# Score tiles as two runs of 64-row products, with a ScalarE copy before their search

## The chip, the core and the metric

The kernel runs on one NeuronCore of a Trainium2 chip. The metric is device time in microseconds of one execution. Five engines work side by side, each in the order of its own queue: TensorE (PE, matrix products; PEld is its weight load), VectorE (DVE), ScalarE (ACT), GpSimd (POOL) and SyncE (SP, which here issues most DMAs). They wait for each other through semaphores. Products are summed in PSUM, which has eight banks of 128 partitions by 512 fp32 values; everything else lies in SBUF or in DRAM.

## What is computed

The input x is 2048 rows of 512 values. With xn the row-wise normalised x, the output is x + A(xn) + B(xn):

- A is attention with 32 heads of 16 and one shared head of keys and values: scores, softmax over 2048 keys, weighted sum of values, output projection.
- B is a mixture of 4096 tiny experts with product keys: for each row and head, a query gives 64 scores against each of two key sets (k1, k2), the best two of each set are found, their four sums ranked, and the best two experts taken, with a softmax over two as gates. Each expert is one row of u and one row of v: `gelu(xn . u) * gate * v`, summed over heads.

The query weights and the keys are multiplied first, so the expert scores of a row are one product of xn with a 512 x 4096 matrix. Per row that gives 64 groups (32 heads, two sets) of 64 scores.

## The kernel before

**Units of work.** Rows come in 16 tiles of 128, four tiles to a phase (`TPH`). The 4096 score columns come in eight chunks of 512 (`NC`). `SEQ` (line 508) lists the 32 pairs of phase and chunk in the order in which they are scored: phase 0 whole, two chunks of phase 1, phase 2 whole, the rest of phase 1, phase 3 whole. For phases 0 and 1 the experts found are gathered from DRAM (a slot is one gathered expert for each of 128 rows: a dot at line 999, an add at line 1034). For phases 2 and 3 the experts are computed densely by `dense`, once the last chunk of the phase is scored.

**A score tile** is made by `item` (lines 513 to 549): twelve products of 128 contracted rows by 512 columns (four parts of the 512-long contraction, each with three terms of a high and low split), summed in one PSUM tile named psc. The weights are XT (xn transposed, one per phase group) and the moving operand WC (the chunk's matrix, tiles wk). Then VectorE searches the PSUM tile directly: eight MAX8 and eight FIND_INDEX8 (with their MATCH_VALUE_LOAD) over 64 columns each. After four tiles `batch` turns maxima and indices into expert numbers and gates.

**PSUM.** `xtile` (line 123) hands out one-bank tiles from a ring of three, to score tiles and to all other users: wp_make, block_out (pwo), the dense part (pact, pg, pout, ptd). `stile` hands out two pairs of banks for attention scores.

**Order.** From line 1255 on the order on every engine is written out by hand. The loop (line 1259) has 256 steps d, each with four calls of `scores` (attention scores, `sc`, line 327: two products of 64 contracted rows, in the upper and the lower half of the array, into two banks, and one exponential on ScalarE) and two of `pv` (line 341: products with 32 output columns). A step is emitted as: two scores, two pv, `mid` (VectorE's dots and adds, ScalarE's small functions, gathers), two scores, sometimes a `block_out` (four 128-row products of the output projection, pwo), then `fill`. `fill` runs a generator, `score_thread`, until the sum of the costs that it yields reaches a line that ends at FILL after 256 steps; three score products cost 3 x `UNIT` = 0.705. So a step has 15 or 18 score products. The generator also makes the chunks' matrices (`wp_make`, for chunks 0 to 7, done by the seventh chunk); later chunks are read back from DRAM (`wp_read`, tiles wk, eight buffers, two chunks). At a change of phase `load_xt` loads each tile's columns of XT after its last use.

The number of gather slots worked on in a step is set by `pos` (line 1267): 2.1 a step until phase 0 is searched, then 2.3 for twelve steps after a dense part and 1.75 otherwise, with rates of its own in the dense part.

Of the kernel before, what the change touches and what calls it, by code (L numbers as in the profile page):

```python
# [11 lines left out]
F32 = mybir.dt.float32  # L12
# [4 lines left out]
U32 = mybir.dt.uint32  # L17
# [6 lines left out]
P = 128  # L24
# [4 lines left out]
E = 64  # L29
# [3 lines left out]
KC = D // P  # L33
NC = 8
TPH = GT
# [6 lines left out]
NWK = 8  # L42
NIDX = 9
GS = 8192.0
FILL = 948.0
SCALE = DH ** -0.5
LIMIT2 = 25000.0
C_IN = 0.7978845608028654
# [3 lines left out]
UNIT = 0.235  # L52
# [3 lines left out]
def tile_kernel(ctx, tc, x, wq, wkv, wo, wqT, kT, uv, ub, vb, out):  # L56
    nc = tc.nc
# [4 lines left out]
    late = [None]  # L62
    start_stack = ExitStack()
    small = pool("small", bufs=2)
# [55 lines left out]
    nc.gpsimd.memset(ones_f, 1.0)  # L120

    gtile = lambda dt=F32, shape=(P, 1024), name="g": big.tile(list(shape), dt, name=name, tag="g", bufs=NGB)
    xtile = lambda name: ps.tile([P, 512], F32, name=name, tag="x", bufs=3)
    stile = lambda name: ps.tile([P, 2, 512], F32, name=name, tag="s")


# [375 lines left out]
    def wp_read(n, ks=range(KC)):  # L502
        for k in ks:
            wk = wk_tile()
            nc.sync.dma_start(raw(wk[:]), d_w[SEQ[n][1]][:, k])
            WC.setdefault(n, []).append(wk)
# [3 lines left out]
    M8, I8 = {}, {}  # L510
    BT = 4

    def item(n_, ti, make=()):
        ph, c = SEQ[n_]
        nph, nc_ = SEQ[n_ + 1] if n_ + 1 < len(SEQ) else (None, None)
        t = TPH * ph + ti
        g, j = divmod(t, GT)
        b, jb = divmod(ti, BT)
        if jb == 0:
            m8 = small.tile([P, BT, 8, 8], F32, name="m8", bufs=1)  # L520
            i8 = small.tile([P, BT, 8, 8], U32, name="i8", bufs=1)
            M8[ph, c, b], I8[ph, c, b] = m8, i8
        m8, i8 = M8[ph, c, b], I8[ph, c, b]
        p = xtile("psc")

        more = nc_ is not None and not (ph >= NSP and c == NC - 1)
        read = more and n_ + 1 >= NC
        n = 0
        for k in range(KC):
            for a, bb in TERMS:  # L530
                nc.tensor.matmul(p, XT[k][:, a, j * P:(j + 1) * P], WC[n_][k][:, bb, :],  # L531
                                 start=n == 0, stop=n == 11)
                n += 1
            if read and ti == 0 and k < 2:
                wp_read(n_ + 1, range(2 * k, 2 * k + 2))
            if k < KC - 1:
                yield 3 * UNIT
            if k == 1:

                yield from islice(make, 1)  # L540
        if more and nph != ph:
            load_xt(nph, j)
        for s in range(8):
            nc.vector.max(m8[:, jb, s, :], p[:, s * E:(s + 1) * E])  # L544
        for s in range(8):
            nc.vector.max_index(i8[:, jb, s, :], m8[:, jb, s, :], p[:, s * E:(s + 1) * E])  # L546
        if jb == BT - 1:
            batch(ph, c, b)
        yield 3 * UNIT

    IDX, G = {}, {}
# [544 lines left out]
        ACC[t], XN[t] = xa[:, 0, :], xa[:, 1, :]  # L1096
        LIVE.add(t)

    def load_xt(g, j=None, ks=range(KC)):
        c = slice(0, 512) if j is None else slice(j * P, (j + 1) * P)  # L1100
        for k in ks:
            nc.sync.dma_start(raw(XT[k][:, :, c]), d_xt[g - 1][k][:, :, c])

    def score_thread():
        for n, (ph, c) in enumerate(SEQ):
            if n < 2:
                yield from wp_make(c)
            make = wp_make(n + 1) if 0 < n < NC - 1 else iter(())
            dn = None
            if ph >= NSP and c == NC - 1:  # L1110
                dn = dense(ph, n + 1 if n + 1 < len(SEQ) else None)
                yield next(dn)
            for ti in range(TPH):
                if dn and ti == 1:
                    yield next(dn)
                if dn and ti == 2:
                    dense_on[0] = 4
                yield from item(n, ti, make)
                yield from islice(make, 1)
            yield from make  # L1120
            WC.pop(n)
            if ph >= NSP and c == NC - 1:
                yield from dn
                dense_on[0] = 0

# [129 lines left out]
    with tc.manual_schedule(engines={E_.PE, E_.Activation, E_.DVE, E_.Pool, E_.SP}):  # L1255
# [3 lines left out]
        for d in range(half + 24):  # L1259


            if dense_on[0] != 0:
                since = d
            if dense_on[0] == 1:
                pos += 2.6 if d < half * 3 // 4 else max(0.0, NSL - pos) / max(half - 3 - d, 1)
            else:
                pos += (2.1 if len(IDX) < NC * TPH else 2.3 if 0 <= d - since < 12 else 1.75, 0, 1.4, 1.5, 0.5)[dense_on[0]]

            todo = max(min(int(pos + 0.001), g_next[0]) - d_next[0], 0)

# [108 lines left out]
```

## Time and profile before

| | us |
|---|---|
| median of 3 runs | 1915.05 |
| lowest and highest run | 1909.74, 1916.33 |
| the profiled execution | 1918.82 |
| its span, first to last instruction | 1917.1 |

The profiler's record of one execution gives, for each instruction, its engine, its start and its length. Rows of the timeline show the start, the length, the engine, the line of the kernel, what is written and read, and how many equal instructions in a row were merged (x). `64*128` in a TensorE row means 64 contracted rows and 128 columns of the array. Rows of stretches show the start and end, the length, then the busy time and the number of instructions of each engine. Product lengths include the way through the array, so products that follow each other overlap in the record; the distance of their starts is what one costs.

### The profile page before, as it was taken

What the parts mean: (1) busy time and instruction counts of PE and PEld (TensorE: products, weight loads), DVE (VectorE), ACT (ScalarE), POOL (GpSimd) and SP (SyncE); (2) the same over time, 40 slices, a digit from 0 to 9 for tenths busy, and PEclk for the clock granted to TensorE, in tenths of its full rate; (3) what the DMA queues carried; (4) which work ended last, traced back from release to release, by engine and by line L of the source; (5) the groups of instructions that cost most, each with busy time, mean ns of one, the idle gap of its engine ahead of it and who ended that gap; (6) DMA issues with size and microseconds to landing.
All of it is one profiled execution on the core that took longest, in us unless ns stands there. A gap on an engine that the chain in (4) does not pass through costs nothing.

```text
span 1917.1 us, 35007 instructions
## 1 busy us (share of the span) xinstructions
PE 1822.9 (95%) x10990; PEld 961.5 (50%) x10990; DVE 1633.0 (85%) x6381; ACT 1290.6 (67%) x1803; POOL 693.8 (36%) x920
## 2 busy tenths in 40 slices
PE   6879999999999889999999999999998899999998
PEld 4544444555555344555555454555543345555553
DVE  6626888889998987999999797899989779999994
ACT  3236666655557987787877555555579777878773
POOL 1202334334443213343444354344522124444430
PEclk9989999999999999999999999999999899999999
DMA  7856878898673678898999987877646878899982
GB/s 264 312 191 235 293 267 289 286 296 282 232 261 111 223 245 259 250 288 274 284 289 307 340 283 234 290 244 264 229 129 220 263 222 292 267 285 280 295 265 79
DMA packets 245724, 489.76 MB, mean 255 GB/s; under 512 B 93972, under 2 KB 106644, under 8 KB 245532
## 3 DMA queue, kind: packets, MB, share of 16 engines
q0 software_dynamic: 73728, 268.47, 42.1%
q1 hardware_dynamic: 170568, 218.18, 35.0%
q8 instruction: 88, 1.44, 0.3%
q10 hardware_dynamic: 1236, 0.82, 0.1%
q14 instruction: 104, 0.85, 0.1%
HBM read 426.49 MB, written 55.61 MB: 251 GB/s over the span
## 4 chain that ended last, share of the span: by engine, by line
PE 76%; DVE 10%; DMA 3%; ACT 2%; issue 1%; SPq 1%; ACTq 0%; DVEq 0%
PE pv L341 20%; PE psc L531 18%; PE sc L327 15%; PE pact L733 9%; PE pout L872 9%; DVE oh L792 3%; PE pwo L434 2%; DVE xa L1034 2%; DVE g L999 1%; PE pw L487 1%; DVE oh L795 1%; ACT pt L330 1%; DVE oh L794 1%; DMA wqt<-in_wqT_dram 1%; DMA wk<-dw 1%
## 5 line engine op out<-in xcount | busy, mean ns | idle before, releaser
L330 ACT ACTIVATE pt<-sc 128x1024 f32<-128x1024 f32 x1024 | 994.6, 1028 | 449.1 <-PE sc L327 394.2
L987 POOL DMA_INDIRECT g<-in_uv_dram,idx x512 | 555.0, 1084 | 997.1 <-DVE xa L1034 518.3
L341 PE MATMUL pv<-pt,vaug 128*32 128x512 f32 x4096 | 499.4, 604 | 0.0
L327 PE MATMUL sc<-qa,kaug 64*128 64x512 f32 x2048 | 387.7, 451 | 15.7 <-ACT pt L330 14.1
L531 PE MATMUL psc<-wk,xt 128*128 128x512 f32 x1536 | 390.4, 402 | 8.0 <-DMA wk<-dw 4.4
L1034 DVE SCALAR_TENSOR_TENSOR xa<-g,w,xa 128x512 f32<-128x512 f32 x512 | 372.2, 745 | 0.1
L999 DVE CUSTOM_DVE_ANT_0 g<-g,xa 128x512 f32<-128x512 f32 x512 | 335.7, 682 | 6.2 <-DMA g<-in_uv_dram,idx 6.2
L531 PEld LDWEIGHTS psc<-wk,xt 128*128 128x128 f32 x1536 | 278.9, 189 | 111.8 <-issue 39.6
L327 PEld LDWEIGHTS sc<-qa,kaug 64*128 64x128 f32 x2048 | 157.4, 186 | 332.3 <-ACT pt L330 206.5
L341 PEld LDWEIGHTS pv<-pt,vaug 128*32 128x32 f32 x4096 | 107.7, 110 | 247.6 <-issue 246.0
L546 DVE FIND_INDEX8 i<-m,psc 128x8 uint32<-128x64 f32 x1024 | 206.6, 222 | 0.0
L733 PE MATMUL pact<-xt,wk 128*128 128x512 f32 x768 | 196.0, 400 | 0.0
L872 PE MATMUL pout<-wk,wd 128*128 128x512 f32 x768 | 194.9, 402 | 0.2 <-DVE wd L930 0.2
L544 DVE MAX8 m<-psc 128x8 f32<-128x64 f32 x1024 | 146.6, 215 | 41.3 <-PE psc L531 36.8
L872 PEld LDWEIGHTS pout<-wk,wd 128*128 128x128 f32 x768 | 140.8, 188 | 47.5 <-DVE act L999 5.5
L733 PEld LDWEIGHTS pact<-xt,wk 128*128 128x128 f32 x768 | 139.4, 188 | 48.5 <-issue 17.4
L875 DVE TENSOR_TENSOR da<-da,pout 128x512 f32<-128x512 f32 x128 | 82.9, 680 | 10.1 <-PE pout L872 6.6
L698 DVE TENSOR_TENSOR wk<-rw,wk 128x512 fp32r<-128x512 f32 x128 | 84.9, 684 | 6.7 <-ACT wk L697 6.7
L792 DVE TENSOR_TENSOR oh<-oh 128x2048 f16<-128x2048 f16 x64 | 78.0, 1219 | 0.6 <-ACT pt L330 0.4
L697 ACT CAST wk<-rw 128x512 fp32r<-128x512 f32 x128 | 74.1, 632 | 0.0
L546 DVE MATCH_VALUE_LOAD i<-m,psc 128x8 f32 x1024 | 72.6, 71 | 0.0
L1022 DVE SCALAR_TENSOR_TENSOR w<-gth,ga 128x4 f32<-128x4 f32 x128 | 20.5, 160 | 51.2 <-ACT gth L1015 50.6
(159 smaller groups left out, 1344.6 us busy)
## 6 DMA issues: line engine op xcount, KB each, us to landing
wk<-dw SPq DMA_DIRECT2D x96, 512.0 KB
wqt<-in_wqT_dram SPq DMA_DIRECT2D x32, 512.0 KB
dw<-wk SPq DMA_DIRECT2D x32, 512.0 KB
rw<-in_ub_dram SPq DMA_DIRECT2D x64, 256.0 KB
rw<-in_vb_dram SPq DMA_DIRECT2D x64, 256.0 KB
gy<-dg SPq DMA_DIRECT2D x64, 256.0 KB
qa<-dqh SPq DMA_DIRECT2D x128, 64.0 KB
g<-in_uv_dram,idx POOLq DMA_INDIRECT x512
```

Of the source, the lines that this page charges most:

```text
L327: nc.tensor.matmul(p[:, b, :], kaug[o:o + 64, kc * P:(kc + 1) * P], QA[u][o:o + 64, i, :], start=True, stop=True)
L330: nc.scalar.activation(pt, p, AF.Exp, scale=SCALE)
L341: nc.tensor.matmul(PV[u][32 * j:32 * j + 32, :], vaug[:, kc, :], pt[:, b, :], start=kc == 0, stop=kc == 15)
L531: nc.tensor.matmul(p, XT[k][:, a, j * P:(j + 1) * P], WC[n_][k][:, bb, :], start=n == 0, stop=n == 11)
L544: nc.vector.max(m8[:, jb, s, :], p[:, s * E:(s + 1) * E])
L546: nc.vector.max_index(i8[:, jb, s, :], m8[:, jb, s, :], p[:, s * E:(s + 1) * E])
L733: nc.tensor.matmul(p, us[:, a, k * P:(k + 1) * P], XT[k][:, c, :], start=n == 0, stop=n == 11)
L792: nc.vector.tensor_tensor(out=oa, in0=num(P), in1=bc(0, tb, P), op=OP.is_equal)
L872: nc.tensor.matmul(p, wd[0][:, a, j * P:(j + 1) * P], vs[:, c, :], start=n == 0, stop=n == 5)
L987: nc.gpsimd.indirect_dma_start(out=gt, out_offset=None, in_=uv, in_offset=bass.IndirectOffsetOnAxis(ap=IDX[ph, c, ti][:, s:s + 1], axis=0))
L999: nc.vector.tensor_tensor_reduce(u, u, XN[TPH * ph + ti], scale=1.0, scalar=0.0, op0=OP.mult, op1=OP.add, accum_out=a[:, i:i + 1])
L1034: nc.vector.scalar_tensor_tensor(acc, v, w[:, i:i + 1], acc, op0=OP.mult, op1=OP.add)
```

## The change

From the eighth chunk on (`n_ >= NC - 1`, 25 of 32 chunks) a score tile is an object `Halves`. Each of its twelve steps is two products of 64 contracted rows: the first run uses rows 0 to 63 and writes the tile's first sum, the second run uses rows 64 to 127 and adds to it. `first_half` issues a first-run step and queues its partner; once more than 18 (`LAG`) are queued, the oldest partner is issued right behind. So TensorE's queue alternates between a first-run product of one tile and a second-run product of an older tile, in another bank.

Between the runs of a tile stands a small ScalarE copy (`seen`): it waits for the last product of the first run, and the first product of the second run waits for it. At the end of the second run `done` copies the tile to SBUF on ScalarE (`scp`, in the ring of tag wd with four buffers), and the search reads that copy. `xtile` now keeps the owners of its ring of three; before it hands out a buffer whose owner's second run isn't over, it issues second-run products until it is. At the end of the last chunk of phases 2 and 3 the remaining second runs are issued, three to a yield.

`wp_read` for the next chunk moves from the first tile of a chunk to the second one, and `load_xt` at a change of phase is issued in two parts, each of half the rows, after the run that uses them. FILL goes from 948 to 956, and two of the rates of `pos` go down.

```diff
-FILL = 948.0
+FILL = 956.0
...
-    xtile = lambda name: ps.tile([P, 512], F32, name=name, tag="x", bufs=3)
+    RING = [None] * 3
+
+    def xtile(name, owner=None):
+        first = RING.pop(0)
+        while first is not None and not first.over:
+            second_half()
+        RING.append(owner)
+        return ps.tile([P, 512], F32, name=name, tag="x", bufs=3)
...
+    class Halves:
+        def __init__(self, steps, done):
+            self.steps, self.done = steps, done
+            self.p = xtile("psc", self)
+            self.over = False
+
+        def step(self, i, half):
+            w, v = self.steps[i]
+            o = slice(64 * half, 64 * half + 64)
+            mm = nc.tensor.matmul(self.p, w[o], v[o], start=i == 0 and half == 0, stop=i == 11 and half == 1)
+            if half == 0 and i == 11:
+                self.seen = nc.scalar.copy(seen, ident[:, 0:1])
+                tc.add_manual_dep(self.seen.ins, mm.ins.name, SYNC, reason="first rows are summed")
+            if half == 1 and i == 0:
+                tc.add_manual_dep(mm.ins, self.seen.ins.name, SYNC, reason="first rows are summed")
+            if half == 1 and i == 11:
+                self.over = True
+                self.done(self.p)
...
+    SECOND, LAG = [], 18
+
+    def first_half(tile_, i):
+        tile_.step(i, 0)
+        SECOND.append((tile_, i))
+        if len(SECOND) > LAG:
+            second_half()
+
+    def second_half():
+        tile_, i = SECOND.pop(0)
+        tile_.step(i, 1)
+
+    def second_halves():
+        while SECOND:
+            for _ in range(min(3, len(SECOND))):
+                second_half()
+            yield 3 * UNIT
...
+        def done(p):
+            if reload:
+                load_xt(nph, j, rows=slice(64, P))
+            sb = late[0].tile([P, 2, 512], F32, name="scp", tag="wd", bufs=4)[:, 0, :]
+            nc.scalar.copy(sb, p)
+            search(sb)
+
+        if halves:
+            tile_ = Halves(steps, done)
+            for k in range(KC):
+                for i in range(3 * k, 3 * k + 3):
+                    first_half(tile_, i)
+                if read and ti == 1 and k > 1:
+                    wp_read(n_ + 1, range(2 * k - 4, 2 * k - 2))
+                if k < KC - 1:
+                    yield 3 * UNIT
+            if reload:
+                load_xt(nph, j, rows=slice(0, 64))
+            yield 3 * UNIT
+            return
...
             if ph >= NSP and c == NC - 1:
+                yield from second_halves()
                 yield from dn
...
-                pos += (2.1 if len(IDX) < NC * TPH else 2.3 if 0 <= d - since < 12 else 1.75, 0, 1.4, 1.5, 0.5)[dense_on[0]]
+                pos += (2.1 if len(IDX) < NC * TPH else 2.15 if 0 <= d - since < 12 else 1.62, 0, 1.4, 1.5, 0.5)[dense_on[0]]
```

More of the change, by code (lines that the diff above doesn't have):

```diff
@@ L511, in tile_kernel @@
     BT = 4
+    class Halves:
[15 more added lines that the diff above has]
+                self.done(self.p)
+    SYNC = mybir.DependencyInfo(mybir.DependencyClass.Sync, mybir.DependencyReason.DATA)
+    seen = small.tile([P, 1], F32, name="seen", bufs=1)
+    SECOND, LAG = [], 18
[12 more added lines that the diff above has]
+            yield 3 * UNIT
     def item(n_, ti, make=()):
@@ L518, in item, with search @@
         b, jb = divmod(ti, BT)
[L519 to L524, printed above, removed]
         more = nc_ is not None and not (ph >= NSP and c == NC - 1)
         read = more and n_ + 1 >= NC
+        halves = n_ >= NC - 1
+        reload = more and nph != ph
+        steps = [(XT[k][:, a, j * P:(j + 1) * P], WC[n_][k][:, bb, :]) for k in range(KC) for a, bb in TERMS]
+        def search(p):
+            if jb == 0:
+                M8[ph, c, b] = small.tile([P, BT, 8, 8], F32, name="m8", bufs=1)
+                I8[ph, c, b] = small.tile([P, BT, 8, 8], U32, name="i8", bufs=1)
+            m8, i8 = M8[ph, c, b], I8[ph, c, b]
+            for s in range(8):
+                nc.vector.max(m8[:, jb, s, :], p[:, s * E:(s + 1) * E])
+            for s in range(8):
+                nc.vector.max_index(i8[:, jb, s, :], m8[:, jb, s, :], p[:, s * E:(s + 1) * E])
+            if jb == BT - 1:
+                batch(ph, c, b)
+        def done(p):
[17 more added lines that the diff above has]
+            return
+        p = xtile("psc")
         n = 0
         for k in range(KC):
-            for a, bb in TERMS:
-                nc.tensor.matmul(p, XT[k][:, a, j * P:(j + 1) * P], WC[n_][k][:, bb, :],
-                                 start=n == 0, stop=n == 11)
+            for _ in TERMS:
+                nc.tensor.matmul(p, *steps[n], start=n == 0, stop=n == 11)
                 n += 1
@@ L540, in item @@
                 yield from islice(make, 1)
[L541 to L548, printed above, removed]
+        search(p)
         yield 3 * UNIT
@@ L1097, in load_phase2_tile, with load_xt @@
         LIVE.add(t)
-    def load_xt(g, j=None, ks=range(KC)):
+    def load_xt(g, j=None, ks=range(KC), rows=slice(0, P)):
         c = slice(0, 512) if j is None else slice(j * P, (j + 1) * P)
         for k in ks:
-            nc.sync.dma_start(raw(XT[k][:, :, c]), d_xt[g - 1][k][:, :, c])
+            nc.sync.dma_start(raw(XT[k][rows, :, c]), d_xt[g - 1][k][rows, :, c])
     def score_thread():
```

## The prediction

> **What bounds the kernel now.** I read the page first, then TensorE's timeline of one step, then the stretches in which the changed products run.
>
> ```profile
> PE 1822.9 (95%) x10990; PEld 961.5 (50%) x10990; DVE 1633.0 (85%) x6381; ACT 1290.6 (67%) x1803; POOL 693.8 (36%) x920
> ...
> PE 76%; DVE 10%; DMA 3%; ACT 2%; issue 1%; SPq 1%; ACTq 0%; DVEq 0%
> PE pv L341 20%; PE psc L531 18%; PE sc L327 15%; PE pact L733 9%; PE pout L872 9%; DVE oh L792 3%; PE pwo L434 2%; DVE xa L1034 2%; DVE g L999 1%; PE pw L487 1%; DVE oh L795 1%; ACT pt L330 1%; DVE oh L794 1%; DMA wqt<-in_wqT_dram 1%; DMA wk<-dw 1%
> ```
>
> TensorE is busy 95% of the span and has 76% of the chain; 18% of it are the score products of line 531. So the change is priced on TensorE. Its timeline of two steps in chunk nine and after:
>
> ```profile
> 391.78 0.73 PE L327 MATMUL sc<-qa,kaug 64*128 64x512 f32 x4
> 392.44 1.92 PE L341 MATMUL pv<-pt,vaug 128*32 128x512 f32 x16
> 394.29 0.73 PE L327 MATMUL sc<-qa,kaug 64*128 64x512 f32 x4
> 394.96 3.70 PE L531 MATMUL psc<-wk,xt 128*128 128x512 f32 x15
> ```
> ```profile
> 398.26 0.39 PE L531 MATMUL psc<-wk,xt 128*128 128x512 f32 x1
> 398.58 0.73 PE L327 MATMUL sc<-qa,kaug 64*128 64x512 f32 x4
> 399.25 1.92 PE L341 MATMUL pv<-pt,vaug 128*32 128x512 f32 x16
> 401.10 0.73 PE L327 MATMUL sc<-qa,kaug 64*128 64x512 f32 x4
> 401.76 4.38 PE L531 MATMUL psc<-wk,xt 128*128 128x512 f32 x18
> 406.07 0.73 PE L327 MATMUL sc<-qa,kaug 64*128 64x512 f32 x4
> ```
>
> A step is two attention score pairs (sc), sixteen pv products, two more score pairs and a fill of 15 or 18 score-tile products, with no idle time in the rows: 6.80 us with 15 (391.78 to 398.58), 7.49 us with 18. Eighteen take 0.68 us longer than fifteen (4.38 against 3.70), so **one slot is 0.227 us**. The psc block runs from 394.96 to 398.58, 3.62 us; fifteen slots are 3.40, so 0.22 us go to the change of shape. An sc block is 0.66 us (391.78 to 392.44) for two slots of 0.227: 0.21 us again. Each of the four blocks of a step pays about 0.21 us because its neighbour has another array shape (64\*128, 128\*32, 64\*128, 128\*128).
>
> How much of the program is concerned:
>
> ```profile
> 357.70:599.60 241.90, 129.18 (x526) 95.88 (x525) 1.00 0.77 259
> 1064.90:1410.50 345.60, 167.48 (x672) 123.77 (x672) 1.00 0.76 257
> ```
> ```profile
> 357.70:592.80 235.10, 50.08 (x272) 20.39 (x272) 1.00 0.79 266
> 1071.00:1410.50 339.50, 70.62 (x384) 28.66 (x384) 0.99 0.75 255
> ```
>
> Two stretches. The first fence counts line 531: 528 (two records are missing) and 672 products, the 25 chunks of 48 from the eighth on. The second counts line 327: 272 and 384 products, at eight a step 34 and 48 steps. In the second stretch four steps are given to block_out and one to the dense part, so 77 steps have such a fill.
>
> **The change part by part.** *What goes.* The fill becomes 64\*128, the shape of the score pairs on both sides of it. Three blocks become one and pay 0.21 once instead of three times: 0.42 us a step. The 36 extra slots below lengthen the stretches by two fills, so 79 x 0.42 = **-33.2 us**.
>
> *Does a pair of halves fit a slot?* A slot now holds a 64-row product of one tile and one of an older tile, in different rows of the array. Line 327 does this already: two such pairs in 0.66 us, which is the shape price and two slots. I keep 0.227 us; three slots in a row of this kind are not in the trace, so I allow 0.220 to 0.233 for it, 1236 slots, -9 to +7 us.
>
> *Halves that are alone.* The second run starts eighteen steps late, so at the start of each stretch 18 first halves run alone and at its end 18 second halves. Alone, each takes a slot for half the work: 72 slots for the work of 36, so 36 x 0.227 = **+8.2 us**. FILL rises by 8.0, about these 36 x 0.235 in the planner's units.
>
> *The ring.* xtile now ends the oldest tile first if its second run isn't over. Between score tiles alone this costs nothing: a tile is over at slot 29 after its start and its buffer wanted at slot 36. But block_out takes a buffer too, four times in the second stretch:
>
> ```profile
> 1143.10 3.70 PE L434 MATMUL pwo<-wo,on 128*128 128x512 f32 x8
> ...
> 1149.91 3.70 PE L531 MATMUL psc<-wk,xt 128*128 128x512 f32 x15
> ```
>
> With every second step a pwo and 15 slots between, the buffer that is wanted belongs to a tile two starts back, which lacks some six second halves. They run alone, and afterwards as many first halves run alone until the lag is eighteen again. Followed by hand for the four ways in which tiles can lie to the fill this is 39 to 45 of each, so 42 slots, 9.5 us. Their copies come at a bad moment as well; I put 3 us on it (0 to 5). **+12.5 us**.
>
> *The two new hand-offs to ScalarE.* The second run's first product waits for the small copy "seen", which waits for the end of the first run: seven slots are between them. The first product of the third tile after waits for the copy of the finished tile into SBUF: again seven slots. Both copies stand in ScalarE's queue behind the step's exponentials, which this decides:
>
> ```profile
> 392.38 1.94 ACT L330 ACTIVATE pt<-sc 128x1024 f32<-128x1024 f32 x2 [2.35 <-PE sc L327]
> 394.89 1.94 ACT L330 ACTIVATE pt<-sc 128x1024 f32<-128x1024 f32 x2 [0.57 <-PE sc L327]
> ```
> ```profile
> L1015 ACT ACTIVATE gth<-gy 128x4 f32<-128x4 f32 x128 | 27.3, 213 | 0.5 <-DVE gy L1009 0.5
> L488 ACT COPY wt<-pw 128x512 f32<-128x512 f32 x32 | 18.8, 587 | 37.8 <-PE pw L487 37.0 <-issue 0.6
> ```
> ```profile
> 448.47 1.94 ACT L330 ACTIVATE pt<-sc 128x1024 f32<-128x1024 f32 x2 [3.31 <-PE sc L327]
> ```
> ```profile
> 450.46 0.19 PEld L327 LDWEIGHTS sc<-qa,kaug 64*128 64x128 f32 x2 [0.17 <-ACT pt L330]
> ```
>
> Exponentials end at 396.83 (394.89 + 1.94). The copy costs 0.59 us (L488), the small one 0.21 (L1015), each overlapping its predecessor by 0.1 (two exponentials of 1.03 end after 1.94). From ScalarE's end to the weight load are 0.05 us (450.41 to 450.46), and a first product after a stop ends 0.11 later (0.50 instead of 0.39: four sc in 0.73). With the change the fill's slot p starts at 394.29 + 0.11 + 0.45 + 0.227 p = 394.85 + 0.227 p. Fills advance by 15, so hand-offs fall on p = 2, 5, 8, 11 or 14:
> - tile copy asked at p = 2: ends 396.83 + 0.49 = 397.32, product possible at 397.48, wanted at p = 9, 396.89: **0.59 us late**. At p = 5, wanted at 397.57: in time by 0.1.
> - "seen" asked at p = 2: product possible at 397.10, wanted at 396.89: **0.21 late**. Later ones are in time.
> - tile copy asked in the last slot, 398.03: starts 0.49 later as an exponential does after its product (394.40 to 394.89), ends 399.11, and the next exponentials start 0.25 late. The second score pair of the next step had 0.03 us to spare (392.38 + 1.94 + 0.05 = 394.37 against its load at 394.40): **0.23 late**.
>
> Each falls on about one fill in five (every fifth has 18 and shifts the phase): (0.59 + 0.21 + 0.23)/5 = 0.20 us a step, x 79 = **+15.8 us**; between none at all, and 0.59 in every fill, 47 us. I take the timetable.
>
> Sometimes ScalarE is late already, since its tanh waits for VectorE:
>
> ```profile
> 1198.28 3.70 PE L531 MATMUL psc<-wk,xt 128*128 128x512 f32 x15
> ```
> ```profile
> 1199.90 1.93 ACT L330 ACTIVATE pt<-sc 128x1024 f32<-128x1024 f32 x2
> ```
>
> Here the exponentials begin 1.62 us after the fill; in the step above 0.07 before it. Until now the fill hid it; now it delays a hand-off. I put 2 us on it (0 to 8).
>
> *VectorE.*
>
> ```profile
> 357.70:592.80 235.10, 235.10 (x1342) 130.46 (x1341) 220.18 (x1417) 137.33 (x168) 106.93 (x201) 1.00 0.79 266
> ```
> ```profile
> L546 DVE FIND_INDEX8 i<-m,psc 128x8 uint32<-128x64 f32 x352 | 71.0, 222 | 0.0
> L544 DVE MAX8 m<-psc 128x8 f32<-128x64 f32 x346 | 49.6, 215 | 7.0 <-PE psc L531 6.7
> L1034 DVE SCALAR_TENSOR_TENSOR xa<-g,w,xa 128x512 f32<-128x512 f32 x60 | 42.6, 745 | 0.0
> L999 DVE CUSTOM_DVE_ANT_0 g<-g,xa 128x512 f32<-128x512 f32 x60 | 39.8, 680 | 0.0
> ```
>
> It is busy 220.18 of 235.10 us, 6.48 a step. The lower pace (1.62 for 1.75) takes 0.13 x (42.6 + 39.8)/60 = 0.18 from it: 6.30 in a step of 6.59 (6.81 - 0.42 + 0.20), 96%. It follows, barely. Some ten gather slots move to the last dense stretch, where the planner then asks for at most the 2.6 a step that the first dense stretch has today: nothing. ScalarE, 137.33 of 235.10, has room for the copies' time (1.3 x 0.8 a step); only their place hurts. On SP the XT reloads become two of half the rows, same bytes; reads of wk are asked about twenty slots later but their buffers also come free later, and some 25 slots remain.
>
> **Sum:** -33.2 + 8.2 + 12.5 + 15.8 + 2 = +5.3 us. The profiled execution took 1918.82 us with a span of 1917.1; the median is 1915.05, and I set the sum on that: **1920 us**. What can be told from no change is 0.3%, so 1909.3 to 1920.8 is "same"; the forecast lies at its upper edge.
>
> **The rivals.** *B, the hand-offs are covered:* the fills mostly miss p = 2, or ScalarE gets to its copies sooner. Then -33.2 + 8.2 + 9.5 = -15.5: 1900 us. For it: every row of a step repeats to 0.01 us, so luck of phase can last. Against: 15 and 12 share only the factor 3, so the phases rotate.
>
> *C, VectorE becomes the bound (slower):* it now idles 6% of the stretch. If it can't get under that, its step is 6.30/0.94 = 6.70 instead of 6.59, 79 x 0.11 = +9, and each lateness reaches ScalarE's tanh and the hand-offs: with the 8 us of that bound 1920 + 9 + 6 = 1935. It decides once VectorE is more than four tiles behind, when the copy has no buffer (wd has four) and stops the exponentials. Whether a search out of SBUF costs other than out of PSUM no row shows; 215 ns it is from PSUM.
> [...]
>
> *D, wk arrives late:* the stretch begins with such a stop today:
>
> ```profile
> 1077.17 0.96 PE L531 MATMUL psc<-wk,xt 128*128 128x512 f32 x3 [2.81 <-DMA wk<-dw]
> 1079.73 5.12 PE L531 MATMUL psc<-wk,xt 128*128 128x512 f32 x15 [1.60 <-DMA wk<-dw]
> ```
>
> With under 25 slots of notice a read could be late in many chunks; 23 chunks at 0.7 us (a quarter of 2.81) give 1936. Against: no other stop of this size lies in the stretches.
>
> *E, the change doesn't do what it says:* a half's weights load only when its own rows stand still. Then a slot is load and product, 0.19 + 0.227, and 1236 x 0.19 = +235: 2150 us.
>
> ```profile
> 561.15 3.27 PEld L531 LDWEIGHTS psc<-wk,xt 128*128 128x128 f32 x15 [0.36 <-issue]
> ```
>
> Against: fifteen loads of all rows lie in 3.27 us beside their fifteen products.
> [...]
>
> **How the numbers follow.** Forecast case 0.48, own range 1909 to 1931 (slot width and waits of 0.1 to 0.3 us a step): 0.02 faster, 0.24 same, 0.22 slower. B 0.27, all faster. C 0.15, D 0.07, E 0.03, all slower. Together faster 0.29, same 0.24, slower 0.47. From B with a slightly shorter slot to beyond C and D: 1897 to 1938, which leaves E and the tails out.
>
> **What would show it.** In the step: no shape loss between sc and psc, steps with 15 slots of 6.39 to 7.0 us, mean 6.6. Waits of psc on ScalarE's seen and scp copies, some 15 us in all; if under 5, B. Single-half slots in the steps with pwo. VectorE's share in the stretches over 96% would be C, psc waiting for wk D. A pair slot other than 0.227 us would be the mistake that moves most.

## The result, and the profile after

The changed kernel takes **1962.35 us** (median of 4 runs, 1959.44 to 1966.62) against 1915.69 us for the kernel before beside it: a ratio of **1.0258, 95% interval 1.0235 to 1.0281**. A second time, on another chip, it took 1963.59 us (1.0252, 1.0235 to 1.0269). The forecast was 1920 us, +5.3 us; the change costs 47. Its profiled execution has a span of 1964.9 us (1917.1 before).

From the page of the changed kernel: engines' busy time and share, the chain of work that ended last, and the groups that the change made (busy us, mean ns | idle time ahead of them and what ended it).

```profile
PE 1826.4 (93%) x12190; PEld 992.1 (50%) x12190; DVE 1624.2 (83%) x6381; ACT 1359.4 (69%) x2003; POOL 696.4 (35%) x920
...
PE 55%; DVE 20%; DMA 7%; issue 6%; ACT 4%; POOL 1%; SPq 1%; DVEq 0%; ACTq 0%; POOLq 0%
...
L1071 DVE CUSTOM_DVE_ANT_0 g<-g,xa 128x512 f32<-128x512 f32 x512 | 336.2, 683 | 36.6 <-DMA g<-in_uv_dram,idx 35.6
L532 PE MATMUL psc<-wk,xt 64*128 64x512 f32 x2400 | 318.2, 395 | 23.7 <-DMA wk<-dw 12.7
...
L591 ACT COPY scp<-psc 128x512 f32<-128x512 f32 x100 | 59.0, 590 | 58.1 <-PE psc L532 45.6
```

TensorE's share of the chain fell from 76% to 55%; VectorE's doubled to 20%, DMA's went from 3% to 7%. So the path left TensorE, on which the whole prediction was priced. Where? The windows view, cut at the first products of each stage, gives length, then busy time of PE, PEld, DVE, ACT and POOL, the granted clock, DMA share and GB/s. Before and after, the six rows are: first score stretch, dense part, second stretch, dense part up to pout, last dense stretch, end.

```profile
356.80:596.00 239.20, 239.20 (x1370) 131.96 (x1368) 224.28 (x1450) 140.01 (x173) 107.19 (x202) 1.00 0.78 263
596.00:1069.70 473.70, 455.06 (x3031) 239.24 (x3030) 429.27 (x976) 380.99 (x560) 172.44 (x163) 1.00 0.83 264
1069.70:1403.00 333.30, 328.18 (x1834) 177.20 (x1833) 295.74 (x1822) 189.90 (x232) 152.55 (x251) 0.99 0.77 259
1403.00:1552.80 149.80, 132.14 (x1197) 59.60 (x1195) 129.49 (x301) 126.11 (x201) 38.21 (x44) 0.95 0.66 209
1552.80:1882.60 329.80, 329.58 (x1857) 181.06 (x1856) 306.13 (x717) 257.44 (x364) 128.78 (x115) 1.00 0.86 270
1882.60:1917.10 34.50, 27.10 (x98) 9.41 (x96) 9.67 (x16) 8.98 (x10) 0.00 (x0) 0.88 0.18 62
```
```profile
356.00:611.30 255.30, 240.35 (x1897) 145.43 (x1897) 216.48 (x1414) 169.81 (x259) 106.04 (x199) 0.98 0.75 241
611.30:1092.30 481.00, 458.59 (x3029) 239.28 (x3028) 428.50 (x996) 380.68 (x559) 168.93 (x162) 0.99 0.82 257
1092.30:1436.70 344.40, 331.91 (x2530) 195.93 (x2529) 286.00 (x1803) 229.93 (x346) 143.80 (x246) 1.00 0.73 244
1436.70:1581.60 144.90, 123.40 (x1174) 57.70 (x1173) 120.93 (x278) 122.93 (x197) 33.75 (x39) 0.99 0.62 196
1581.60:1931.60 350.00, 335.42 (x1858) 182.74 (x1856) 324.54 (x772) 258.79 (x367) 147.72 (x130) 0.99 0.87 277
1931.60:1964.90 33.30, 24.96 (x98) 8.13 (x96) 9.78 (x16) 8.95 (x10) 0.00 (x0) 0.99 0.19 63
```

Differences, row by row: **+16.1, +7.3, +11.1, -4.9, +20.2, -1.2** (and -0.8 ahead of them), together +47.8. The second stretch has one attention step more than before and the part behind it one less, so these two belong together: +6.2. The largest item, 20 us, lies in a stage in which no product was changed. The two stretches with the part behind them, which the forecast's sum had at +5.3 us (and at -15.5 with the hand-offs covered), lost 22.3.

The products themselves do what was forecast. TensorE's timeline of the changed kernel:

```profile
469.71 0.63 PE L335 MATMUL sc<-qa,kaug 64*128 64x512 f32 x4
470.26 1.92 PE L349 MATMUL pv<-pt,vaug 128*32 128x512 f32 x16
472.12 0.73 PE L335 MATMUL sc<-qa,kaug 64*128 64x512 f32 x4
472.69 3.77 PE L532 MATMUL psc<-wk,xt 64*128 64x512 f32 x30
476.10 0.82 PE L335 MATMUL sc<-qa,kaug 64*128 64x512 f32 x4
```

The step is 6.39 us long (476.10 - 469.71; 6.80 before), and thirty halves take 3.41 us (472.69 to 476.10): 0.227 us a pair, with no price of shape on either side of the fill. But few steps are like this one: of the changed kernel's 81 distances between steps in the two stretches 15 are under 6.45 us, and the middle ones are 6.98 and 6.93, where the kernel before has 6.81 in both.

### The profile page after: what moved, and what is told of

Read it like the earlier page. It is cut to its first block, busy times and chain, and to the rows that moved or that the text cites. A ratio compares the mean times of both kernels' runs of the same rounds, so it can differ in the third digit from the quotient of the medians.

```text
span 1964.9 us, 37548 instructions
## 1 busy us (share of the span) xinstructions
PE 1826.4 (93%) x12190; PEld 992.1 (50%) x12190; DVE 1624.2 (83%) x6381; ACT 1359.4 (69%) x2003; POOL 696.4 (35%) x920
## 4 chain that ended last, share of the span: by engine, by line
PE 55%; DVE 20%; DMA 7%; issue 6%; ACT 4%; POOL 1%; SPq 1%; DVEq 0%; ACTq 0%; POOLq 0%
PE pv L349 15%; PE psc L532 13%; PE sc L335 10%; PE pact L805 5%; PE pout L944 5%; DVE xa L1106 4%; DVE g L1071 4%; PE psc L611 3%; DVE oh L864 3%; ACT pt L338 3%; DMA wk<-dw 2%; DMA g<-in_uv_dram,idx 2%; PE pwo L442 2%; PE pw L495 1%; DMA rw<-in_vb_dram 1%
## 5 line engine op out<-in xcount | busy, mean ns | idle before, releaser
L532 PE MATMUL psc<-wk,xt 64*128 64x512 f32 x2400 | 318.2, 395 | 23.7 <-DMA wk<-dw 12.7
L335 PEld LDWEIGHTS sc<-qa,kaug 64*128 64x128 f32 x2048 | 173.1, 186 | 314.0 <-ACT pt L338 216.0
L532 PEld LDWEIGHTS psc<-wk,xt 64*128 64x128 f32 x2400 | 243.2, 185 | 83.1 <-issue 13.4
L944 PE MATMUL pout<-wk,wd 128*128 128x512 f32 x768 | 198.7, 405 | 11.3 <-DVE gy L987 8.0
L581 DVE MAX8 m<-scp 128x8 f32<-128x64 f32 x800 | 110.8, 211 | 64.1 <-ACT scp L591 57.4
L583 DVE FIND_INDEX8 i<-m,scp 128x8 uint32<-128x64 f32 x800 | 157.9, 220 | 0.0
L591 ACT COPY scp<-psc 128x512 f32<-128x512 f32 x100 | 59.0, 590 | 58.1 <-PE psc L532 45.6
L611 PE MATMUL psc<-wk,xt 128*128 128x512 f32 x336 | 91.9, 409 | 3.6 <-DVE wk L505 3.6
L611 PEld LDWEIGHTS psc<-wk,xt 128*128 128x128 f32 x336 | 58.8, 188 | 36.0 <-issue 19.4
```

Of the source, the lines that this page charges most:

```text
L335: nc.tensor.matmul(p[:, b, :], kaug[o:o + 64, kc * P:(kc + 1) * P], QA[u][o:o + 64, i, :], start=True, stop=True)
L532: mm = nc.tensor.matmul(self.p, w[o], v[o], start=i == 0 and half == 0, stop=i == 11 and half == 1)
L611: nc.tensor.matmul(p, *steps[n], start=n == 0, stop=n == 11)
L944: nc.tensor.matmul(p, wd[0][:, a, j * P:(j + 1) * P], vs[:, c, :], start=n == 0, stop=n == 5)
```

## The experiments

Three theories stood after the comparison. **Pace:** the planner's lower numbers push gather slots into the last dense stretch, which can't carry them. **SP:** the XT reloads in halves double SP's transfers, and the reads of wk behind them come late. **Hand-offs:** the halves wait for ScalarE, by the timetable or because ScalarE is behind VectorE. Against all three stood the rival that halves simply cost what is lost.

### Pace and SP, alone and together (one chip, e1 to e4)

e1 puts only the two numbers into the kernel before; e2 takes them out of the changed one:

```diff
- (2.1 if len(IDX) < NC * TPH else 2.3 if 0 <= d - since < 12 else 1.75, 0, ...
+ (2.1 if len(IDX) < NC * TPH else 2.15 if 0 <= d - since < 12 else 1.62, 0, ...
```

> The kernel before, with only the planner's two numbers of the change (2.15 and 1.62 gather slots a step where 2.3 and 1.75 stood; score tiles, copies and reloads as before). Pace theory: the slots that these numbers push out of the two stretches come back in the last dense stretch, whose gathers can't be fetched faster, so it takes about 20 us longer there (330 to 350 us) and the stretches gain nothing: about 1935 us. Rival (the halves themselves cost, the pace is free): within 5 us of the kernel before, and the last dense stretch stays at 330 us.

> The changed kernel with the pace of before (2.3 and 1.75). Pace theory: the last dense stretch goes back from 350 to about 332 us, the two score stretches lose at most 4 us to a busier VectorE: about 1946 us. Rival (VectorE can't carry the old pace beside halves, so the lower numbers pay for themselves): the stretches lose 10 us or more and the total stays within 5 us of the changed kernel.

e3 reloads XT in one piece, in the changed kernel; e4 is e2 and e3 together:

```diff
         def done(p):
             if reload:
-                load_xt(nph, j, rows=slice(64, P))
+                load_xt(nph, j)
...
-            if reload:
-                load_xt(nph, j, rows=slice(0, 64))
             yield 3 * UNIT
```

> The changed kernel with each XT reload in one piece of 128 rows after the tile's second run, 16 transfers at a change of phase instead of 32. SP theory: SP is free some 9 us sooner at each of the three changes of phase, the reads of wk go out in time, the stop of 6.1 us at 404 goes to under 1 us, and stretch 1 is 8 to 13 us shorter, stretch 2 some 3: about 1950 us. Rival (the reads are late because the buffers come free late, not because of SP's queue): the stops stay, within 3 us of the changed kernel; the reload itself, asked 18 slots later, could be waited for and make it 5 us slower.

> Both edits together: pace of before and whole XT reloads in the changed kernel. If pace and SP are separate causes, the gains add: about 1934 us, still some 18 us over the kernel before, the cost of the halves. If one cause stands behind both (VectorE late), they don't add: about 1945 us.

The kernel before took 1914.25 us on this chip, and by its ratio the changed one stands at 1963.6.

| kernel | us | ratio to before, 95% | first stretch | second | last dense |
|---|---|---|---|---|---|
| e1, before with the low pace | 1934.77 | 1.0111 (1.0094 to 1.0128) | 239.0 | 327.9 | 343.7 |
| e2, after with the old pace | 1952.86 | 1.0196 (1.0176 to 1.0215) | 255.4 | 348.1 | 330.9 |
| e3, after with whole XT | 1956.95 | 1.0216 (1.0191 to 1.0241) | 246.4 | 341.7 | 348.4 |
| e4, both | 1946.00 | 1.0152 (1.0123 to 1.0181) | 246.3 | 347.6 | 330.4 |

**The two numbers alone cost the kernel before 20.5 us** by the medians, without a single half in it. (The two profiled executions are 14.6 us apart, 13.9 of it in the last dense stretch.) In the changed kernel they cost 11 (e3 against e4: 1956.95 and 1946.00): 18 in the last dense stretch, while in these profiles the second stretch is 6 us shorter with the low pace (341.7 against 347.6). **Reloads in halves cost 7 us** (e2 against e4: 6.9; the changed kernel against e3: 6.7); the first stretch alone is 9 us longer with them. Together the two add up: 1963.6 - 10.7 - 6.7 = 1946.2, measured 1946.0. So they act as separate causes. The 1934 us expected of e4 in that case was missed because each edit gave less than expected (e2 and e3 had been put at 1946 and 1950 us), and e4 still stands 31.8 us over the kernel before.

Both effects stay put across the runs. The last dense stretch takes 343.7 to 352.3 us in the five kernels with the low pace (347.8 in e11) and 329.7 to 333.8 in the eight with the old one. The first stretch takes 253.1 to 257.5 us in the four profiles with halves and halved reloads, and 243.2 to 246.4 in the five with halves and whole ones at the same LAG.

Where the pace costs is the last dense stretch. Windows of that stage, of e1, of e4 and of e3:

```profile
1555.00:1898.70 343.70, 333.15 (x1856) 182.32 (x1854) 321.74 (x765) 258.04 (x367) 162.53 (x128) 0.99 0.88 280
```
```profile
1579.70:1910.10 330.40, 329.72 (x1857) 180.82 (x1856) 309.98 (x730) 257.39 (x365) 131.81 (x118) 1.00 0.88 273
```
```profile
1572.50:1920.90 348.40, 334.09 (x1857) 181.87 (x1856) 324.40 (x772) 258.44 (x367) 146.69 (x130) 0.99 0.88 278
```

In this stage the trace counts 119 gather dots before, 131 after, 130 in e1 and 120 in e4. A slot is a dot (0.68 us) and an addition (0.74) with small change, 1.5 us; twelve are 18 us, and VectorE's busy time rises by 18.4 (306.13 to 324.54). Stage less VectorE's busy time is 23.7 us before, 22.0 in e1, 25.5 after, 24.0 in e3, 20.4 in e4. TensorE, which before stood still for 0.2 us of the stage, now does so for 14.6, most of it waiting for VectorE's results. In the kernel before VectorE already had 93% of the stage (306.13 of 329.80). So one reading is that the room for twelve slots wasn't there. Another is that their gathers come late: VectorE's waits for gathers are 1.9 us before, 0.4 in e4, 14.2 in e1, 19.3 in e3 and 20.0 in the changed kernel, nearly what each stage is longer than before (0.6, 13.9, 18.6, 20.2). e11 below tries to tell the two apart. The granted clock (0.99 against 1.00) is worth some 3 us at most, by an estimate: 1% of the stage.

### XT halves in the kernel before (e5)

```diff
         if more and nph != ph:
-            load_xt(nph, j)
+            load_xt(nph, j, rows=slice(0, 64))
+            load_xt(nph, j, rows=slice(64, P))
```

> The kernel before, with only its XT reloads cut into two of 64 rows each (asked at once, one behind the other): 32 transfers at a change of phase instead of 16, the same bytes. SP theory: SP needs 9 us more at each change of phase, and wk's reads come 9 us later than the four slots of notice that the kernel before has beyond them: 3 to 10 us slower, as stops of psc on wk behind the changes of phase. Rival (what is late in the changed kernel is not SP's count of transfers but the later release of the wk buffers): within 2 us of the kernel before.

1920.53 us against 1914.73: **1.0030 (1.0015 to 1.0044)**, 5.8 us, and the first stretch takes 245.9 us instead of 239.2, as the SP theory had it. The mechanism is to be seen in SP's own rows; first the reloads of the kernel before, then of the changed one (ns min/median/max of one transfer on SP, first and last start), both from 356 to 470 us:

```profile
L1102 SPq DMA_DIRECT2D xt<-dxt x32: 517/562/3162, 362.6 to 423.9; - x32
```
```profile
L1174 SPq DMA_DIRECT2D xt<-dxt x64: 512/552/1760, 360.5 to 447.2; - x64
```

Half the rows take the same 0.55 us on SP. SP's timeline at the first change of phase: the kernel before, e5, and the changed kernel, where the reads of wk go out in two pairs:

```profile
366.90 12.77 SPq L1102 DMA_DIRECT2D xt<-dxt  x11
379.71 2.03 SPq L505 DMA_DIRECT2D wk<-dw  x4
```
```profile
366.45 23.72 SPq L1103 DMA_DIRECT2D xt<-dxt  x26
390.21 2.49 SPq L505 DMA_DIRECT2D wk<-dw  x4
```
```profile
367.61 29.14 SPq L1174 DMA_DIRECT2D xt<-dxt  x26
396.81 1.18 SPq L513 DMA_DIRECT2D wk<-dw  x2
398.08 0.57 SPq L367 DMA_DIRECT2D dsum<-e  x1
398.70 3.29 SPq L373 DMA_DIRECT2D ot<-e  x4
402.03 2.44 SPq L513 DMA_DIRECT2D wk<-dw  x2
```

In the kernel before eleven transfers of XT stand there and all four reads go out from 379.71; in e5, behind 26 transfers, they go out from 390.21. In the changed kernel they begin at 396.81, and TensorE, which wants them from 398.14 on, stands 6.1 us until 404.27, when the first of them has landed. Of the 29.14 us of the 26 transfers some 14 are their own time (26 x 0.55). In most of the rest SP waits before a transfer: between 366 and 397 us 10.6 us until earlier transfers have landed and 4.2 for TensorE. So 26 transfers held SP for 29.14 us (23.72 in e5), where the eleven of the kernel before held it for 12.77. In e5 the products of the first stretch, which before never stood still, do so for 4.1 us. The stop of 6.1 us is gone in e3, whose whole reload, asked 18 steps later, is itself waited for once. Waits of TensorE in the first stretch, changed kernel and e3 (us in all, times, longest):

```profile
PE psc L532 <- DMA wk<-dw: 8.3, 3, 6.1
```
```profile
PE psc L532 <- ACT scp L591: 3.0, 5, 2.0
PE psc L532 <- DMA xt<-dxt: 2.8, 1, 2.8
```

### The copy alone (e6)

```diff
+        sb = p
+        if n_ >= NC - 1:
+            sb = late[0].tile([P, 2, 512], F32, name="scp", tag="wd", bufs=4)[:, 0, :]
+            nc.scalar.copy(sb, p)
+        p = sb
         for s in range(8):
```

> The kernel before, with only the copy: from the eighth chunk on ScalarE copies each finished tile into SBUF and VectorE searches there; products in one run of 128 rows, buffers and pace as before. Hand-off theory (the copy costs only because the bank is wanted seven slots later; here it is wanted 24 slots later): within 3 us of the kernel before. Rival (the copies load ScalarE and delay the exponentials whenever they are asked): 100 copies of 0.49 us in front of exponentials, a fifth to a half of them felt: 8 to 25 us slower.

1912.58 us, **0.9990 (0.9977 to 1.0002)**: the hundred copies cost nothing when the bank isn't wanted for 24 slots. So ScalarE's time for the copies isn't what costs. That the short notice of the halves does, as the hand-off theory has it, is what is left; this kernel, which has neither halves nor "seen" copies, doesn't show it by itself. (And the copy is no gain either.)

### VectorE relieved in the stretches (e7)

```diff
- ... 2.15 if 0 <= d - since < 12 else 1.62, 0, ...
+ ... 1.0, 0, ...
```

with the whole XT reload of e3.

> The changed kernel with whole XT reloads and a pace of 1.0 gather slots a step in both stretches, so that VectorE has some 0.9 us less a step there; the total will be far over (the rest of the slots comes in the last dense stretch) and only the two stretches are read, against 246.5 and 341.7 us with 2.15 and 1.62. If the hand-offs are late because ScalarE waits for VectorE (tanh behind the dots, the copy behind the search), the stretches lose most of their stops: about 234 and 331 us. If it is the timetable alone, they stay within 4 us.

Total 2066.91 us, as it must be (467.5 us for the last dense stretch). The two score stretches, e3 and e7:

```profile
355.50:601.90 246.40, 236.34 (x1896) 144.24 (x1896) 216.54 (x1414) 169.37 (x259) 107.00 (x199) 1.00 0.76 249
1085.00:1426.70 341.70, 331.11 (x2529) 197.22 (x2528) 286.15 (x1803) 229.79 (x346) 141.97 (x246) 1.00 0.73 246
```
```profile
356.10:599.30 243.20, 236.07 (x1897) 144.46 (x1897) 192.20 (x1338) 168.94 (x254) 85.47 (x181) 1.00 0.65 214
1086.80:1420.60 333.80, 329.46 (x2529) 199.04 (x2528) 240.80 (x1664) 229.25 (x337) 99.55 (x211) 0.99 0.60 199
```

VectorE has 24 and 45 us less to do, and the stretches get 3.2 and 7.9 us shorter, **11 us** together: less than the 23 of the one theory, and in the second stretch more than the 4 of the other. Even so relieved, the first stretch (243.2) isn't below the 239.2 of the kernel before. The way from VectorE to these 11 us isn't shown. Fewer slots are also fewer gathers (DMA share 0.65 instead of 0.76 in the first stretch), and in the changed kernel's two stretches ScalarE's rows have only 2.6 us of waiting for VectorE (a copy for a search 1.7, a tanh 0.9). Nor are 3.2 and 7.9 us clear of what one stretch varied by between profiles (e12 below).

### The distance of the two runs (e8)

`SECOND, LAG = [], 16` instead of 18, on top of e4.

> Pace of before and whole XT reloads in the changed kernel, with the second run 16 steps behind instead of 18: nine slots for the copy, five for seen, and two slots fewer alone at each end. Against 1946.0 us with 18: timetable theory: seen comes late more often than the copy is relieved, +2 to +6 us. If the copy is what is mostly late (its waits were the larger), -3 to -8 us.

1952.82 us, 1.0195 (1.0177 to 1.0214) against e4's 1.0152 on another chip: 6.8 us by the medians, 8 by the ratios. The direction is the timetable's, a little more than it said: giving to the copy what is taken from "seen" doesn't pay.

### Halves in the first stretch alone (e9)

`halves = NC - 1 <= n_ < 2 * NC + 2`, on top of e4. The chunks of the second stretch then go by the path of the first seven, which has no XT reload, so this kernel leaves out the 16 transfers at that stretch's change of phase.

> Pace of before and whole XT reloads in the changed kernel, and halves only in the first stretch; the chunks of the second go in one run of 128 rows, searched out of PSUM, as before. If each stretch pays for itself: the first stretch stays at 246 us, the second goes back to 328 to 334 us with one step less, and the dense stages between and behind lose what the halves' late ends brought them only once: about 1928 us. If the loss behind the first stretch (8 us in the dense stages between) comes from the first stretch's halves, it stays; if from something else, it goes and the time is about 1920 us.

1937.02 us, 1.0115 (1.0078 to 1.0151), over both expectations. First stretch 245.5, second 328.7 with one step less, as the first case had it; the dense part between still takes 7 us more than before, so that loss comes with the first stretch's halves. But the last dense stretch and the end are 4 and 7 us longer, which the expectation had not counted. Probably the planner's FILL, left at 956, now runs the dense work a step ahead.

### More room for finished tiles (e10)

```diff
-            sb = late[0].tile([P, 2, 512], F32, name="scp", tag="wd", bufs=4)[:, 0, :]
+            if not SPARE:
+                w = late[0].tile([P, 2, 512], F32, name="scp", tag="wd", bufs=4)
+                SPARE.extend((w[:, 1, :], w[:, 0, :]))
+            sb = SPARE.pop()
```

on top of e4.

> Pace of before and whole XT reloads in the changed kernel, and the copies of two tiles share one SBUF buffer, so that up to seven finished tiles can wait for VectorE instead of four. Where ScalarE's copy waits for a search (three times, 5.0 us of its idle time), it stands before the exponentials and TensorE follows. If those stops are a main part of the stretches' waits: 5 to 12 us under 1946.0 us. If ScalarE's place in the timetable and tanh's wait for VectorE make most of them: within 3 us.

1944.88 us, 1.0154 (1.0122 to 1.0186), the same as e4, though the copies' waits for a search (5.0 us in e4) are gone. The copy's four buffers are not the limit. The expectation's other case, the timetable and tanh's wait for VectorE, is left by this, not shown.

### A gentler start of the last dense stretch (e11), and the changed kernel again (e12)

Profiles showed VectorE waiting in this stage for gathers that had not landed, changed kernel first, then before:

```profile
DVE g L1071 <- DMA g<-in_uv_dram,idx: 20.0, 13, 4.1
```
```profile
DVE g L999 <- DMA g<-in_uv_dram,idx: 1.9, 2, 1.1
```

That gave a rival to VectorE's lack of room: ten gather buffers that can't turn over so fast at the start. e11 spreads the same slots otherwise:

```diff
- ... max(0.0, NSL - pos) / max(half - 3 - d, 1)
+ ... min(2.4 if d < 219 else 9.0, max(0.0, NSL - pos) / max(half - 3 - d, 1))
```

> The changed kernel (its lower pace too), with the planner held to 2.4 gather slots a step in the first twelve steps of the last dense stretch, and the rest spread over the steps after them (some 3.0 a step instead of 2.8). The same 131 slots are left for this stretch. Buffer theory (ten gather buffers, each held 28 to 35 us from its gather to its add there, pass 2.0 to 2.4 slots in a step of 6.9 us; asking for 2.8 at once makes VectorE stand before gathers that have not landed, and TensorE behind it): the waits for gathers of 20 us in the first 80 us fall below 6, the stretch takes 335 to 342 us instead of 350, the total about 1952 us. Rival (the twelve slots cost because VectorE has no room for their 18 us, wherever they lie): the stretch stays at 347 to 352 us.

The waits for gathers fell to 11.3 us, not below 6, and the stage still took 347.8 us, with VectorE busy for 324.49: inside the rival's bounds. **The buffer theory is weakened**: 8.7 us less of waiting for gathers gave 2.2 us of stage. It isn't excluded, since the waits were only halved. And room alone isn't all of it either: in e7's last dense stretch, with 183 dots, VectorE was busy for 393.51 of 467.50 us and waited 69.0 for gathers. That the moved slots make the stage longer is shown; by which of the two ways stays open.

The total of 1947.14 us (1.0198, 1.0165 to 1.0231) is 11 us lower by its ratio than the changed kernel's, more than the stage explains. The second score stretch took 332.2 us, though up to the last dense stretch both kernels are one program. So the changed kernel ran again:

> The changed kernel as it is, a second time on another chip, to tell what of the difference to the run with the ramp is the ramp's: up to the last dense stretch both are one program, and yet the second score stretch took 344.4 us in the one profile and 332.2 in the other. If the stretches with halves vary by themselves (small waits that fall together or not): the second stretch lies anywhere between 330 and 346 us, the last dense stretch stays at 349 to 351, the ratio within 0.5% of 1.0258. If the ramp did it after all: 344 us again and a ratio of 1.0235 to 1.028.

1963.59 us, 1.0252; first stretch 257.5, second 341.8, last dense 352.3. In the last dense stretch two to four microseconds are the ramp's. Why the second stretch took some 10 us less in e11's profile is not settled: this result fits both cases of the expectation about equally well. It isn't the chance of one execution, for all four runs of e11 (at most 1951.90) lie under all eight of the changed kernel (at least 1959.44). So between three profiles of what is one program up to there the first stretch varied by 4 us and the second by 12, and a difference of that size between two profiles, e7's among them, proves little.

## Why the prediction was wrong, point by point

**Shape and slot: right.** -0.41 us in an undisturbed step (6.80 - 6.39; 0.42 forecast) and 0.227 us a pair, by the rows above. Rival E is out: it had load and product one behind the other, 0.19 + 0.227 us a slot, and both kernels took 0.227 a slot, beside loads of 0.188 us (128 rows, line 531 before) and 0.184 (64 rows, line 532 after; medians).

**Halves alone and the ring: right in size.** Nine halves alone at 1177.90 last 2.25 us; less the 0.39 of one record that is 0.23 for each of eight, a whole slot as forecast. The ring, by windows of psc's instructions over the eight steps with block_out, before and after:

```profile
1139.91:1195.10 55.19, 16.06 (x64) 11.52 (x63) 14.95 (x130) 1.00 0.69 224
```
```profile
1157.85:1219.35 61.50, 19.88 (x126) 15.64 (x125) 0.00 (x0) 2.98 (x5) 1.00 0.60 202
```

The same work (64 products, 126 halves) takes 6.3 us longer, where shape alone gives 3.4 back: 9.7 us, other stops in these steps included, against 12.5 forecast.

**Hand-offs: foreseen, but mis-sized.** Idle time of line 532 in the whole changed kernel, by what ended it:

```profile
  DMA wk<-dw: 21.7, 12
  issue: 18.0, 15
  ACT scp L591: 11.5, 25
  ACT seen L534: 7.7, 10
```

The 19.2 us on the two copies look like the forecast (15.8 and the ring's 3), but these rows add the idle time of loads and of products: the products alone stood 2.9 us for the large copy and 2.7 for "seen". Some of "issue" is the copies' too (at 1136.10 a load that starts just behind the copy's end is booked there), and some is the 6.1 us stop for wk a second time. Rows of idle time also miss short stops: a product's record lasts 0.39 us and a product costs 0.227, so a stop under 0.16 us leaves none.

An estimate from the undisturbed step gets around this. Without its fill that step takes 2.98 us (469.71 to 472.69). The first stretch has 35 steps and 546 slots (510 pairs, 36 halves alone): 35 x 2.98 + 546 x 0.227 = 228. The second has 48 steps, 732 slots with the forecast's 84 alone for the ring, and four blocks of pwo at 3.63 us (1163.97 to 1167.60 in the changed kernel): 324. What a kernel takes beyond these 552 us it stood still: 48 us in the changed kernel, 42 in e4, 36 in e3, 25 in e7. The kernel before, worked out likewise, stood some 7. So the change brought some 41 us of stops, 34 without SP's 7 (below). The forecast had 20.8 (0.20 us a step, 15.8, the ring's 3 and 2 for ScalarE's lateness): **the terms for the hand-offs were too small by some 13 us**. In e7, with VectorE relieved, it is 18, and those terms would have been enough.

**VectorE "follows, barely": open.** By the prediction's own sign, a share over 96%, rival C did not happen: VectorE had 85% and 83% of the two stretches (216.48 of 255.30 us, 286.00 of 344.40). Nor do the full tile buffers that C named cost anything (e10). But the stops get fewer as VectorE has less to do (42 us in e4, 36 in e3, 25 in e7), so its load, or that of the gathers which goes with it, may make part of them: up to 11 us by e7, where 2 were in the sum. It is not shown, since by the same estimate e11, with the lower pace and halved reloads of the changed kernel, has 33 where that has 48.
The prediction had no row on what a search out of SBUF costs. Measured, MAX8 and FIND_INDEX8 are cheaper there by 4 and 2 ns, 211 and 220 against 215 and 222 out of PSUM:

```profile
L581 DVE MAX8 m<-scp 128x8 f32<-128x64 f32 x800 | 110.8, 211 | 64.1 <-ACT scp L591 57.4
L583 DVE FIND_INDEX8 i<-m,scp 128x8 uint32<-128x64 f32 x800 | 157.9, 220 | 0.0
```

**SP, "same bytes": failed.** The step counted bytes, but SP's time went by the number of transfers: 0.55 us for either size, and a wait for earlier ones. 7 us (e2 to e5). Rival D had the symptom, psc waiting for wk, but with the wrong reason, short notice of the buffers.

**The pace, "some ten gather slots move ... nothing": failed, and worst.** Twelve slots moved, about as said, and the last dense stretch grew by 20 us, 18 to 19 of them by the pace (e3 less e4, the changed kernel less e2), or the full 1.5 us for each slot. The step compared the rate asked (2.6 a step) with that of the first dense stretch, instead of reading VectorE's share in the last one and asking what its gathers can bear.

**The dense parts: not foreseen.** +7.3 us between the stretches, there in e2, e3, e4 and e9 at either pace (7 to 9 us) and not in e1, e5 and e6, which have no halves (1 to 3). Some 5 of the 7 lie ahead of the first pout product, 154.9 us behind the first pact one instead of 149.8. In what way the first stretch's end brings it was argued only (search and gates of the last tiles end a step later); it stays open.

Together, by stage: the two stretches with the part behind them lost 22.3 us where 5.3 were forecast, 7 of the 17 between by SP and some 10 (13 by the estimate above) by more stops than forecast, whose cause is open; the last dense stretch lost 20.2, the dense part between 7.3, and the ends gained 2. That is the 47.8 of the profiles. All rivals sat inside the two stretches; the two misses that are shown, pace and SP, were edits outside the products, costed at nothing. No version with halves beats the kernel before.

## What to carry to other kernels

Work that a planner moves is not saved: price it in the stage where it arrives, by the share of each engine in that stage, not by the rate that another stage bears. Count the transfers of a queue, not only their bytes: here cutting one into two of half the size doubled its own time on SP (0.56 us whole, 2 x 0.55 in halves), and the reads of wk that stood behind it in program order came late (from 390.21 us instead of 379.71 in e5). Measure many short stops by the distance of starts, not by rows of idle time. An edit costed at nothing deserves its own row of the profile, as much as the one that was the point of the change.

## What the runs showed of the hardware

- A transfer of 64 rows of XT held SP for 0.552 us in the changed kernel, one of 128 rows for 0.562 in the kernel before (medians of 64 and 32, from 356 to 470 us).
- Sixty-four-row products in different halves of the array ran fifteen pairs in a row at 0.227 us a pair (changed kernel, 472.69 to 476.10 us), as much as one 128-row product took in the kernel before; their thirty loads, 0.184 us each, lay beside them in 3.57 us.
- Three profiles (changed kernel, e12, e11) of what is one program up to that point gave 344.4, 341.8 and 332.2 us for the second score stretch, a stage of many short waits. What makes the difference is not known.
- MAX8 and FIND_INDEX8 over 64 columns took 211 and 220 ns out of SBUF (changed kernel), 215 and 222 ns out of PSUM (kernel before).
